# Attention, MoE 1 and MoE 2 in one kernel: MoE 2's first pass takes its weights straight from the conversion, with eight units a round and four raw buffers for a group of MoE 1's weights

## The chip, the cores and the metric

One core of a Trainium2 chip runs the whole program. The metric is the device time in microseconds of one execution. Three runs of the kernel before took 927.72, 929.70 and 931.07 us; the median is 929.7.

## The reference

Three layers run one after the other on 4 x 576 = 2304 tokens of width 512. Inputs q, k and v are float32; all weights are float64.

```
scores = q @ k.T / 8 ; half of the heads see a local window of 32, half every 32nd position
x = softmax(masked scores) @ v                       # attention, 8 heads of 64
h = x @ w_in ; x = (h * tanh(softplus(h))) @ w_out   # MoE 1, Mish, inner width 2048
g = x @ w_gate ; out = (silu(g) * (x @ w_val)) @ w_out   # MoE 2, SwiGLU, inner width 1536
```

## The kernel before, in words

**Precision.** Every large matmul is done three times (`mm3`, line 138): weights and activations are split into a high part w[:, 0] and a low part w[:, 1], and high x high, high x low and low x high are added up in PSUM.

**Conversion of a weight.** A float64 weight tile of 128 x 512 arrives as 64-bit integers (a *raw* tile, 512 KB, loaded by SyncE in `w_load`, line 213). `w_ops` (line 274) turns it into float32 with four VectorE steps a, b, c, d; ScalarE takes a Square beside them, which sends tiny values to zero. Then ScalarE casts the high part (`w_hi` or `hi_item`) and VectorE subtracts to get the low part (`w_lo` or `lo_item`). This is a *raw unit*. A *sum unit* (S12 or S34) adds and subtracts two weight tiles in two half-width VectorE steps and is split in the same way. MoE 2's tiles (keys of three parts: kind g, v or p, round, and W0, W1, S12 or S34) are written to DRAM (`wd`) after the split, and `ld` (line 1098) loads them for each round that uses them.

**Products.** With two token chunks of 512, a pass computes its products by a scheme of seven block products (`PROD`, line 683) with operands B11, T1, T2, B22, T3, B21, T4 and the weight tiles W0, S12, S34, W1. The Ts are differences of activation blocks. TensorE writes a bank, ScalarE copies products 0 to 2 aside (line 947 or 1147), and later products add to the same bank.

**MoE 1** goes through four quarters of its inner width. In quarters 1 to 3 (`middle`, line 1020) the order is: `in_round` of the first chunk pair, `small_h` of the small chunk, then `y_phase` of the two chunks (2A+1, 2A) and of the small one; then `in_round` of the second pair and its two `y_phase`. The T operands are made once in quarters 0 and 1 and written to DRAM (`td`); in quarters 2 and 3 `t_load` (line 1091) brings back those of the second pair before its `in_round`: it is issued on POOL's queue, T1 and T2 after the first quarter of the second large and of the small `y_phase`, T3 after the small one. Partial outputs are added up in DRAM (`yd`) by POOL's queue.

**What sets the order.** In attention, the list `ORDER`. In `middle`, a planner: `plan` holds the conversion units in order, with gates that say when a buffer comes free, and `fill` (line 855) emits them on VectorE wherever the engines' model clocks leave room; `need` forces a unit that TensorE is about to use. A unit's split is emitted within the next unit (`with_split`). In quarter q the plan holds four output weights of q, then some units of MoE 2 (`W2_QUARTER`), then the input weights of q + 1 with their sums. Raw tiles have two buffers (tag `raw`); each load is issued when a tile has been used. Conversions of MoE 2 write into two tiles of tag `ws`, which come free when their write to DRAM has landed.

**MoE 2** has rounds 0 to 5 on chunks 0 and 1 and the small chunk, and rounds 6 to 11 on chunks 2 and 3 (line 1318). A round is `c_round` (seven products for g and v), the output tiles of the round before (`d_tile`), and in the first six `c4_round`. 30 of the 60 conversion units of MoE 2 are left for its own rounds (`LATE_ROUND`): `w_late_step` emits one step of them after each group of matmuls. They write into four tiles of tag `wx`, go to DRAM and come back by `ld`. Their two raw tiles (`rawl`) are one half each of a tile that becomes free when MoE 1's last `in_round` is done.

Of the kernel before, what the change touches and what calls it, by code (L numbers as in the profile page):

```python
# [7 lines left out]
F32 = mybir.dt.float32  # L8
# [48 lines left out]
W2_QUARTER = (5, 5, 10, 10)  # L57
LATE_ROUND = (7, 7, 7, 8, 1)
# [46 lines left out]
def local_strided_attention__mish_moe__swiglu_kernel(  # L105
# [51 lines left out]
    w2list = []  # L157
    for i in range(NP):
        for k, kind in enumerate("gv"):
            w2list += [((kind, i, "W0"), w2[2 * i, :, k]), ((kind, i, "W1"), w2[2 * i + 1, :, k])]  # L160
            w2list += [((kind, i, "S12"), None), (("p", i, k), w2[2 * i + k, :, 2]), ((kind, i, "S34"), None)]
    wlist, plan = [], []

    def put_raw(kind, f):
        wlist.append(((kind, f), w1[f, :, "io".index(kind)]))
        plan.append(("unit",))
# [38 lines left out]
    late = {"first": len(wlist), "raw": None, "loads": 0, "units": 0}  # L205
# [7 lines left out]
    def w_load():  # L213
        i = wpos[0]
        while i < len(wlist) and wlist[i][1] is None:
            i += 1
        if i >= late["first"] and late["raw"] is None:
            return
        if i < len(wlist):
# [54 lines left out]
    def w_ops():  # L274
# [11 lines left out]
        else:  # L286
            t = sb.tile([128, 512], I32, tag="pt", name="wt2", bufs=5)
# [24 lines left out]
        raw = raws.pop(i).bitcast(I32).rearrange("p (n t) -> p n t", t=2)  # L312
        lo, hi = raw[:, :, 0], raw[:, :, 1]
        f32[key] = tf
        sq = w[:, 1].bitcast(F32) if len(key) == 2 else sb.tile([128, 512], F32, tag="sq", name="sq")
# [1137 lines left out]
```

## Time and profile before

| | before |
|---|---|
| median of three runs | 929.7 us |
| profiled execution | 927.34 us |
| span in the profile | 925.6 us |
| TensorE matmul / weight load busy | 867.8 / 715.1 us |
| VectorE / ScalarE / POOL busy | 608.0 / 455.3 / 186.6 us |
| moved by DMA | 185.47 MB, 200 GB/s in the mean |

The profile is one execution on the chip. Some 1.7 us of its time lie outside the span. PE is TensorE's matmuls, PEld its weight loads (beside them), DVE is VectorE, ACT ScalarE, SP SyncE. A queue letter (SPq, POOLq) stands for issued DMAs. L141 is line 141, the helper that emits all large matmuls, so such groups are told apart by their tiles: cX, cZ and cY are product banks, y and o output banks, h hidden ones. The clock column is the granted clock of TensorE as a share of 2.4 GHz.

### The profile page before, as it was taken

Reading aid. Unit: us, or ns where it says so; the run is one execution under the profiler, and the core shown is the slowest. Engines: PE = TensorE matmul, PEld = TensorE weight load, DVE = VectorE, ACT = ScalarE, POOL = GpSimd, SP = SyncE. Lnnn points to the kernel's source line nnn. Section 1 sums busy time; section 2 is a strip of 40 time slices with the busy share of each in tenths; the row PEclk is TensorE's granted clock in tenths of the full one; section 3 lists DMA queues with packets and bytes.
Section 4 is the critical chain, followed back from the end, with each engine's and each line's share of the span. In section 5 each row is a group of like instructions: output and inputs, shape, how many; then the busy total and the mean of one; then the engine's idle time right before and its main releaser. Section 6 shows DMA issues by size and latency. Waiting matters only on the chain.

```text
span 925.6 us, 14469 instructions
## 1 busy us (share of the span) xinstructions
PE 867.8 (94%) x5216; PEld 715.1 (77%) x5216; DVE 608.0 (66%) x1334; ACT 455.3 (49%) x1095; POOL 186.6 (20%) x216
## 2 busy tenths in 40 slices
PE   8999999989978879999795799999999999999998
PEld 5778779868856668778584678878888888888886
DVE  6998697767855746775454888978845554334434
ACT  7999846745735436564463553443424423322230
POOL 5633301001000010101113422202123321112211
PEclk9999999999998999999899799999999999999999
DMA  9855236448670495827969697898843466534422
GB/s 288 257 190 187 87 137 250 163 115 200 251 159 27 112 324 219 204 73 211 308 243 289 197 337 266 304 335 320 319 163 97 154 232 201 163 132 159 159 91 91
DMA packets 53351, 185.47 MB, mean 200 GB/s; under 512 B 5792, under 2 KB 9504, under 8 KB 50976
## 3 DMA queue, kind: packets, MB, share of 16 engines
q1 hardware_dynamic: 46512, 152.88, 47.8%
q0 software_dynamic: 6624, 31.46, 13.4%
q8 instruction: 41, 0.67, 0.3%
q14 instruction: 30, 0.25, 0.1%
q10 hardware_dynamic: 144, 0.21, 0.1%
HBM read 123.19 MB, written 61.34 MB: 199 GB/s over the span
## 4 chain that ended last, share of the span: by engine, by line
PE 63%; issue 23%; DMA 6%; DVE 4%; POOL 2%; ACT 2%; SPq 0%; POOLq 0%; DVEq 0%; ACTq 0%
PE o L141 15%; PE y L141 9%; PE cXv L141 6%; PE cXg L141 6%; PE h L141 6%; PE cZg L141 3%; PE cZv L141 3%; PE c L141 3%; PE cX L141 2%; DMA rawl<-in_w_dram 2%; PE cYg L141 2%; PE cYv L141 2%; DMA wd_v_S<-ws 1%; PE tp L501 1%; PE xp L537 1%
## 5 line engine op out<-in xcount | busy, mean ns | idle before, releaser
L141 PE MATMUL y<-g,w 128*128 128x512 f32 (+1 forms) x960 | 205.8, 372 | 8.4 <-DVE w L136 4.7
L141 PEld LDWEIGHTS y<-g,w 128*128 128x128 f32 x960 | 167.3, 190 | 41.0 <-DVE w L136 6.8
L141 PE MATMUL o<-wr,fs 128*128 128x512 f32 x648 | 149.6, 389 | 0.0
L141 PEld LDWEIGHTS o<-wr,fs 128*128 128x128 f32 x648 | 121.3, 188 | 25.0
L136 POOL TENSOR_TENSOR fs<-k,fs 128x512 fp32r<-128x512 f32 x36 | 48.8, 1355 | 252.4 <-ACT fs L131 190.5
L1211 DVE TENSOR_TENSOR acc<-acc,o 128x512 f32<-128x512 f32 x90 | 61.1, 684 | 40.2 <-PE o L141 40.2
L1006 POOL DMA_DIRECT2D yd<-yv x28 | 23.1, 823 | 310.2 <-ACT yv L1000 309.9
L136 DVE TENSOR_TENSOR ws<-wt,ws 128x512 fp32r<-128x512 f32 x60 | 43.8, 731 | 47.6 <-ACT ws L131 46.2
L131 ACT CAST ws<-wt 128x512 fp32r<-128x512 f32 x60 | 37.0, 616 | 64.3 <-DMA wd_g_W<-ws 19.2
L131 ACT CAST fs<-k 128x512 fp32r<-128x512 f32 x36 | 22.4, 622 | 85.5 <-DVE k L1164 40.6
L141 PE MATMUL h<-xh,w 128*128 128x512 f32 (+1 forms) x208 | 61.5, 360 | 0.0
L455 ACT ACTIVATE pt<-pt,sm 128x64 f32<-128x64 f32 (+1 forms) x160 | 55.8, 360 | 4.7 <-DVE sm L441 4.6
L141 PE MATMUL cXg<-T,wr 128*128 128x512 f32 x216 | 55.1, 390 | 1.9 <-ACT k L1147 1.9
L141 PE MATMUL cXv<-T,wr 128*128 128x512 f32 x216 | 54.8, 389 | 0.0
L141 PE MATMUL cX<-xT,w 128*128 128x512 f32 x144 | 41.3, 443 | 12.4 <-DMA xT<-td0T 6.2
L1000 ACT COPY yv<-y 128x512 f32<-128x512 f32 x56 | 31.5, 590 | 36.8 <-PE y L141 31.8
L141 PEld LDWEIGHTS cXg<-T,wr 128*128 128x128 f32 x216 | 40.4, 188 | 11.2 <-ACT k L1147 2.7
L141 PEld LDWEIGHTS cX<-xT,w 128*128 128x128 f32 x144 | 31.8, 223 | 20.8 <-ACT k L947 13.2
L141 PEld LDWEIGHTS cXv<-T,wr 128*128 128x128 f32 x216 | 40.5, 188 | 8.5
L1150 DVE TENSOR_TENSOR k<-cZg,k 128x512 f32<-128x512 f32 x12 | 8.3, 692 | 53.5 <-PE cZg L141 53.5
L141 PEld LDWEIGHTS h<-xh,w 128*128 128x128 f32 x208 | 37.0, 189 | 5.4 <-issue 0.4
L1147 ACT COPY k<-cXg 128x512 f32<-128x512 f32 x24 | 14.2, 590 | 48.0 <-PE cXg L141 48.0
(176 smaller groups left out, 1799.2 us busy)
## 6 DMA issues: line engine op xcount, KB each, us to landing
raw<-in_w_dram SPq DMA_DIRECT2D x50, 512.0 KB, 4.5
yd<-yv POOLq DMA_DIRECT2D x28, 512.0 KB, 7.1
wr<-wd_g_S SPq DMA_DIRECT2D x24, 512.0 KB, 4.0
wr<-wd_v_S SPq DMA_DIRECT2D x24, 512.0 KB, 5.1
wr<-wd_p SPq DMA_DIRECT2D x24, 512.0 KB, 4.7
wr<-wd_g_W SPq DMA_DIRECT2D x18, 512.0 KB, 5.3
wr<-wd_v_W SPq DMA_DIRECT2D x18, 512.0 KB, 5.9
rawl<-in_w_dram SPq DMA_DIRECT2D x18, 512.0 KB, 7.5
```

The lines of the kernel that those rows point to most:

```text
L131: nc.scalar.copy(hi, src)
L136: eng.tensor_tensor(out=lo, in0=src, in1=hi.bitcast(F32), op=ALU.subtract)
L141: nc.tensor.matmul(o, lhsT=lhs, rhs=rhs, start=first and i == 0, stop=last and i == 2, skip_group_check=more)
L455: nc.scalar.activation(out=pt[:, x], in_=pt[:, x], func=AF.Exp, scale=-1.0, bias=sm[:, 0, x:x + 1], accum_out=sm[:, 1, x:x + 1],)
L501: nc.tensor.transpose(tp[:, 128 * x:128 * x + 128], a, ident)
L537: nc.tensor.matmul(banks[r][64 * h:64 * h + 64, o:o + nq - skip], lhsT=v_t[s][rows, i, 64 * h:64 * h + 64], rhs=ts[rows, c0 + skip:c0 + nq ...
L1000: on_act(COPY if nt == 512 else 0.4, clk["pe"], lambda: nc.scalar.copy(dst, p[:, :nt]))
L1006: nc.gpsimd.dma_start(yd[c][:, e0:e + 1], src, **kw)
L1147: nc.scalar.copy(t, p)
L1150: nc.vector.tensor_tensor(out=t, in0=p, in1=t, op=ALU.add)
L1211: nc.vector.tensor_tensor(out=acc[c][:, t], in0=acc[c][:, t], in1=o, op=ALU.add)
```

## The change

MoE 2's units in MoE 1's quarters go from (5, 5, 10, 10) to (5, 2, 8, 9), and those left for its own rounds from (7, 7, 7, 8, 1) to (4, 8, 8, 8, 8). The list is put in another order: before MoE 2 begins come g and v of round 0, g of round 1 and all twelve output tiles p; left are v of round 1 and g and v of rounds 2 to 5, 18 raw units and 18 sum units. These write straight into the tiles that the next round uses (`w2_slot`): S12 and S34 have one tile for each kind, W0 and W1 two in turn by the round's parity. They still go to DRAM for the second six rounds, but `ld` doesn't load them in the first six. `w_late_flush` empties what is left at the head of a round.

Raw tiles of MoE 1's weights get four buffers for a group: the first two of tag `raw`, the other two in `ws`; such a load is issued only when all MoE 2 units before it have been split and written. Loads are now issued at the end of a unit, up to four at once (`w_load(4)`). In a group of input weights, both sums of a column pair now follow that pair.

The T loads go from POOL's queue to ScalarE's: T1 after the third quarter of the first large `y_phase`, T2 and T3 after the first and third quarter of the second. The two late raw loads are issued right after MoE 1's last `in_round`, ahead of the accumulators and of round 0's weights. Operand T4 of the first six rounds is made within MoE 1's last `y_phase` and not after round 0's first product; B11 of the second six after the first product of round 5. In attention, Square comes one step earlier, and the tiles of tag `pt` (five) and `sq` become `pt` (four) and `px` (two).

```diff
-W2_QUARTER = (5, 5, 10, 10)
-LATE_ROUND = (7, 7, 7, 8, 1)
+W2_QUARTER = (5, 2, 8, 9)
+LATE_ROUND = (4, 8, 8, 8, 8)
...
+    def w2_in(kind, i, *what):
+        k = "gv".index(kind)
+        src = {"W0": w2[2 * i, :, k], "W1": w2[2 * i + 1, :, k]}
+        return [((kind, i, x), src.get(x)) for x in what]
+
+    def w2_out(*fs_):
+        return [(("p", f // 2, f % 2), w2[f, :, 2]) for f in fs_]
+
+    w2list = w2_in("g", 0, "W0", "W1", "S12") + w2_out(0) + w2_in("g", 0, "S34") + w2_out(1, 2)
+    w2list += w2_in("v", 0, "W0", "W1", "S12") + w2_out(3) + w2_in("v", 0, "S34") + w2_out(*range(4, 11))
+    w2list += w2_in("g", 1, "W0", "W1", "S12") + w2_out(11) + w2_in("g", 1, "S34")
+    for i in range(1, NP):
+        for kind in "gv"[i == 1:]:
+            w2list += w2_in(kind, i, "W0", "W1", "S12", "S34")
...
+    def put_raw(kind, f, tag="raw"):
+        rtag[len(wlist)] = tag
...
-            put_raw("o", q * QF + f)
+            put_raw("o", q * QF + f, ("raw", "ws")[f // 2])
         if q == 1:
             plan += [("gate", ("in", 1, 0)), ("T", 1, 0), ("T", 1, 1)]
+        if q == 1:
+            n_t1 = len(wlist)
         put_w2(W2_QUARTER[q])
...
-                put_raw("i", (q + 1) * QF + 2 * cp)
-                put_raw("i", (q + 1) * QF + 2 * cp + 1)
-                put_sums(q + 1, *[("S34", 0)] * cp, ("S12", cp))
-            put_sums(q + 1, ("S34", 1))
+                put_raw("i", (q + 1) * QF + 2 * cp, ("raw", "ws")[cp])
+                put_raw("i", (q + 1) * QF + 2 * cp + 1, ("raw", "ws")[cp])
+                put_sums(q + 1, ("S12", cp), ("S34", cp))
...
+    def w_load(most=1):
+        while most:
+            i = wpos[0]
+            while i < len(wlist) and wlist[i][1] is None:
+                i += 1
+            if i >= len(wlist):
+                return
             if i < late["first"]:
-                raws[i] = sb.tile([128, 512], I64, tag="raw", name="raw", bufs=2)
+                tag = rtag.get(i, "raw")
+                if sum(rtag.get(x, "raw") == tag for x in raws) >= 2:
+                    return
+                if tag == "ws":
+                    if any(len(k) == 3 and k not in whole for k, _ in wlist[:i]):
+                        return
+                    if any(("x", P, "T4") not in whole for P in range(2 if i > n_t1 else 1)):
+                        return
+                raws[i] = sb.tile([128, 512], I64, tag=tag, name="raw", bufs=2)
             else:
+                if late["raw"] is None or late["loads"] - late["used"] >= 2:
+                    return
                 raws[i] = late["raw"][:, late["loads"] % 2]
                 late["loads"] += 1
             nc.sync.dma_start(raws[i], wlist[i][1])
-        wpos[0] = i + 1
+            wpos[0] = i + 1
+            most -= 1
...
-            tag, n = ("ws", 2) if i < late["first"] else ("wx", 4)
-            return sb.tile([128, 2, 512], F32R, tag=tag, name="ws", bufs=n)
+            if i >= late["first"]:
+                return w2_slot(key[0], key[1], key[2])
+            return sb.tile([128, 2, 512], F32R, tag="ws", name="ws", bufs=2)
...
         def a():
+            if i < n0:
+                nc.scalar.activation(out=sqo, in_=hi.bitcast(F32), func=AF.Square)
...
             wpend.append((key, w, tf))
-            w_load()
+            del raws[i]
+            if i >= late["first"]:
+                late["used"] += 1
+            if i < n0 or i >= late["first"]:
+                w_load()
...
     def w_late():
         late["raw"] = sb.tile([128, 2, 512], I64, tag="xl3", name="rawl")
-        w_load()
-        w_load()
+        w_load(2)
...
-                ops.insert(len(ops) // 2, w_hi)
-                ops.insert(len(ops) - 1, lambda: w_lo(nc.vector))
+                ops.insert(1 if len(ops) == 2 else 2, w_hi)
+                ops.insert(len(ops) - (len(ops) > 3), lambda: w_lo(nc.vector))
...
+    def w_late_flush():
+        while wq or late["units"] or wpend:
+            w_late_step()
...
         def close():
             key, w, tf = wpend.pop(0)
             behind.append((key, w, tf, lambda: end[0]))
+            w_load(4)
...
             def after1(i):
                 if i < 2:
                     late_g(q, A, i)
+                if i == 2 and q > 1:
+                    t_load(Z, "T1")
 
             def after0(i):
                 if i < 2:
                     g_make(q * NCH + 4, [2 * i, 2 * i + 1], *sm[q, i])
-                if i == 0 and q > 1:
-                    t_load(Z, "T1")
-
-            def after4(i):
-                if i == 0 and q > 1:
-                    t_load(Z, "T2")
+                if i % 2 == 0 and q > 1:
+                    t_load(Z, ("T2", "T3")[i // 2])
 
             def after3(i):
                 if i < 2:
@@ -1068,41 +1105,54 @@
 
             y_phase(q, 2 * A + 1, (0, 2, 1, 3), after1)
             y_phase(q, 2 * A, (0, 2, 1, 3), after0)
-            y_phase(q, 4, (0, 1, 2, 3), after4)
-            if q > 1:
-                t_load(Z, "T3")
+            y_phase(q, 4, (0, 1, 2, 3))
             in_round(q, Z)
             if last:
+                w_late()
                 for c in (0, 1):
                     new_acc(c, 4, 512)
                     nc.sync.dma_start(acc[c], yd[c])
-                ld(0, "S34", "W0", "S12")
+                w2_tiles("w", 6, *[(x, 0, k) if x == "W0" else (x, k) for x in ("W0", "S12", "S34") for k in "gv"])
+                ld(0, "W0", "S12", "S34")
             y_phase(q, 2 * Z + 1, (0, 2, 1, 3), after3)
             if last:
                 drain()
                 new_acc(4, 4, 256)
                 nc.sync.dma_start(acc[4], yd[4])
+                w2_tiles("ws", 2, ("W1", 0, "g"), ("W1", 0, "v"))
+                w2_tiles("raw", 2, ("p", 0), ("p", 1))
                 ld(0, "W1", 0, 1)
-                y_phase(q, 2, (0, 2, 1, 3), lambda i: [operand(0, k) for k in (("B11", "T1"), ("T2", "B22"), ("T3",), ("B21",))[i]])
+                at = (("B11", "T1"), ("T2", "B22"), ("T3", "B21"), ("T4",))
+                y_phase(q, 2, (0, 2, 1, 3), lambda i: [operand(0, k) for k in at[i]])
+                w2_tiles("wx", 4, ("W0", 1, "g"), ("W0", 1, "v"), ("W1", 1, "g"), ("W1", 1, "v"))
...
     def t_load(P, k):
         t_tile(P, k)
-        nc.gpsimd.dma_start(tops[P][k].bitcast(F32), td[P, k])
-
-    ws = {}
-    TAGS = {"W0": ("w", 6), "S12": ("w", 6), "S34": ("w", 6), "W1": ("ws", 2), 0: ("raw", 2), 1: ("raw", 2)}
-
-    def ld(r, *what):
+        nc.scalar.dma_start(tops[P][k].bitcast(F32), td[P, k])
+
+    w2t = {}
+
+    def w2_tiles(tag, n, *names):
+        for x in names:
+            w2t[x] = sb.tile([128, 2, 512], F32R, tag=tag, name="wr", bufs=n)
+
+    def w2_slot(kind, r, x):
+        if kind == "p":
+            return w2t[("W0", 0, "gv"[x]) if r == 2 * NP - 1 else ("p", x)]
+        return w2t[(x, r % 2, kind) if x[0] == "W" else (x, kind)]
+
+    def ld(r, *what, kinds="gv"):
         if r >= 2 * NP:
             return
         P, i = divmod(r, NP)
         for x in what:
-            for kind in "p" if x in (0, 1) else "gv":
-                tag, n = TAGS[x] if kind != "p" or r < 2 * NP - 1 else ("wx", 4)
-                ws[kind, r, x] = t = sb.tile([128, 2, 512], F32R, tag=tag, name="wr", bufs=n)
+            for kind in "p" if x in (0, 1) else kinds:
+                t = w2_slot(kind, r, x)
+                if kind != "p" and P == 0 and i > (kind == "g"):
+                    continue
...
         middle()
-        w_late()
         for r in range(2 * NP + 1):
             P = r // NP
-            late["units"] += LATE_ROUND[r] if r < len(LATE_ROUND) else 0
             if r in (2, 3):
                 new_acc(r, 4, 512)
                 nc.sync.dma_start(acc[r], yd[r])
             if r < 2 * NP:
+                w_late_flush()
+                late["units"] += LATE_ROUND[r] if r < len(LATE_ROUND) else 0
                 ld(r + 1, "W0")
 
                 def between(n):
-                    if r == 0 and n == 0:
-                        operand(0, "T4")
                     if r == 0 and n == 3:
                         small_operand()
                     if n == 2:
                         ld(r + 1, "S12")
                     if n == 4:
                         ld(r + 1, "S34")
-                    if r == NP - 2 and n == 6:
+                    if r == NP - 1 and n == 0:
                         operand(1, "B11")
                     if r == NP - 1 and n in (1, 3):
                         operand(1, ("T1", "T2")[n // 2])
```

## Rows read from the trace of the kernel before

**Rows 1.** Table by stage (start:end, us; busy us per engine; clock; DMA; GB/s).
```profile
163.22:222.47 59.25, 54.65 (x276) 46.07 (x276) 42.93 (x70) 32.39 (x59) 5.17 (x7) 0.97 0.49 135
...
263.30:297.57 34.27, 25.14 (x85) 18.32 (x84) 16.73 (x31) 16.30 (x28) 1.56 (x2) 0.85 0.30 65
297.57:335.54 37.97, 34.19 (x194) 29.29 (x193) 22.72 (x39) 15.54 (x29) 4.59 (x6) 1.00 0.60 175
335.54:384.96 49.42, 43.17 (x182) 35.12 (x181) 35.33 (x61) 27.53 (x51) 3.33 (x5) 0.93 0.79 245
384.96:441.00 56.04, 53.77 (x278) 44.92 (x277) 37.22 (x64) 31.43 (x56) 6.04 (x8) 1.00 0.55 149
441.00:490.45 49.45, 43.29 (x182) 35.33 (x181) 29.01 (x45) 25.38 (x47) 8.35 (x9) 0.93 0.83 268
490.45:532.96 42.51, 27.72 (x133) 23.07 (x132) 25.55 (x33) 17.88 (x33) 15.94 (x14) 0.84 0.79 241
...
611.07:651.15 40.08, 38.74 (x194) 32.73 (x193) 34.34 (x58) 16.84 (x31) 8.02 (x7) 1.00 0.90 334
```
**Rows 2.** Chain of waits, pieces without a stop (start, length, what).
```profile
129.93 10.88 PE y L141 x48
140.81 5.75 PE h L141 x48
```
**Rows 3.** Waits of TensorE in the whole span (total us, times, longest).
```profile
PE cZg L141 <- ACT k L1147: 13.9, 1, 13.9
PE cZ L141 <- ACT w L131: 8.2, 4, 3.4
PE cX L141 <- DMA xT<-td0T: 6.2, 1, 6.2
PE cX L141 <- DMA xT<-td1T: 6.2, 1, 6.2
PE y L141 <- DVE w L136: 4.7, 4, 1.5
```
**Rows 4.** Timeline of SyncE's queue, 468 to 500 us (start, length, what).
```profile
470.41 1.01 SPq L1078 DMA_DIRECT2D acc<-yd  x2
...
496.51 1.04 SPq L225 DMA_DIRECT2D rawl<-in_w_dram  x2
```
**Rows 5.** Timeline of ScalarE, 436 to 511 us (in brackets: idle before, releaser).
```profile
436.72 0.62 ACT L131 CAST ws<-wt 128x512 fp32r<-128x512 f32 x1 [8.37 <-DMA wd_g_W<-ws]
...
510.32 0.67 ACT L323 ACTIVATE sq<-rawl 128x512 f32<-128x512 f32 x1 [12.93 <-DMA rawl<-in_w_dram]
```
**Rows 6.** Timeline of VectorE, 251 to 275 us and 410 to 414 us.
```profile
251.22 0.42 DVE L319 TENSOR_SCALAR wt<-raw 128x512 int32<-128x512 int32 x1
...
272.35 0.42 DVE L300 TENSOR_TENSOR wt<-wt 128x256 f32<-128x256 f32 x1
...
274.41 0.68 DVE L136 TENSOR_TENSOR w<-wt,w 128x512 fp32r<-128x512 f32 x1
...
410.01 0.42 DVE L319 TENSOR_SCALAR wt<-raw 128x512 int32<-128x512 int32 x1
...
413.20 0.42 DVE L319 TENSOR_SCALAR wt<-raw 128x512 int32<-128x512 int32 x1
```
**Rows 7.** Timeline of POOL, 430 to 450 us.
```profile
440.25 0.89 POOL L1093 DMA_DIRECT2D xT<-td1T  x1
```
**Rows 8.** DMA issues of the whole span (count, KB each, median us to landing).
```profile
raw<-in_w_dram SPq DMA_DIRECT2D x50, 512.0 KB, 4.5
...
wd_g_W<-ws SPq DMA_DIRECT2D x12, 512.0 KB, 8.1
...
xT<-td1T POOLq DMA_DIRECT2D x3, 1024.0 KB, 13.7
```

More of the change, by code (lines that the diff above doesn't have):

```diff
@@ L154, in new_acc @@
         acc[c] = sb.tile([128, a, n], F32, tag=f"acc{c}", name=f"acc{c}")
[L157 to L164, printed above, removed]
+    def w2_in(kind, i, *what):
[10 more added lines that the diff above has]
+            w2list += w2_in(kind, i, "W0", "W1", "S12", "S34")
+    wlist, plan, rtag = [], [], {}
+    def put_raw(kind, f, tag="raw"):
+        rtag[len(wlist)] = tag
         wlist.append(((kind, f), w1[f, :, "io".index(kind)]))
@@ L199, in local_strided_attention__mish_moe__swiglu_kernel @@
             for cp in range(2):
-                put_raw("i", (q + 1) * QF + 2 * cp)
-                put_raw("i", (q + 1) * QF + 2 * cp + 1)
-                put_sums(q + 1, *[("S34", 0)] * cp, ("S12", cp))
-            put_sums(q + 1, ("S34", 1))
+                put_raw("i", (q + 1) * QF + 2 * cp, ("raw", "ws")[cp])
+                put_raw("i", (q + 1) * QF + 2 * cp + 1, ("raw", "ws")[cp])
+                put_sums(q + 1, ("S12", cp), ("S34", cp))
     assert len(w2list) == sum(LATE_ROUND)
-    late = {"first": len(wlist), "raw": None, "loads": 0, "units": 0}
+    late = {"first": len(wlist), "raw": None, "loads": 0, "used": 0, "units": 0}
     wlist += w2list
@@ L211, in local_strided_attention__mish_moe__swiglu_kernel @@
     wpos = [0, 0]
[L213 to L219, printed above, removed]
-            if i < late["first"]:
-                raws[i] = sb.tile([128, 512], I64, tag="raw", name="raw", bufs=2)
-            else:
+    whole = set()
+    def w_load(most=1):
[5 more added lines that the diff above has]
+                return
+            if i < late["first"]:
+                tag = rtag.get(i, "raw")
[7 more added lines that the diff above has]
+                raws[i] = sb.tile([128, 512], I64, tag=tag, name="raw", bufs=2)
+            else:
+                if late["raw"] is None or late["loads"] - late["used"] >= 2:
+                    return
                 raws[i] = late["raw"][:, late["loads"] % 2]
@@ L286, in w_ops @@
         else:
-            t = sb.tile([128, 512], I32, tag="pt", name="wt2", bufs=5)
+            t = sb.tile([128, 512], I32, tag="pt", name="wt2", bufs=4)
             tf = t.bitcast(F32)
@@ L311, in w_ops @@
             return [s1, s2]
-        raw = raws.pop(i).bitcast(I32).rearrange("p (n t) -> p n t", t=2)
+        raw = raws[i].bitcast(I32).rearrange("p (n t) -> p n t", t=2)
         lo, hi = raw[:, :, 0], raw[:, :, 1]
         f32[key] = tf
-        sq = w[:, 1].bitcast(F32) if len(key) == 2 else sb.tile([128, 512], F32, tag="sq", name="sq")
-        sqo = w[:, 1] if len(key) == 2 else sq
+        if len(key) == 2 or i >= late["first"]:
+            sq, sqo = w[:, 1].bitcast(F32), w[:, 1]
+        else:
+            sq = sqo = sb.tile([128, 512], F32, tag="px", name="sq", bufs=2)
         def a():
+            if i < n0:
+                nc.scalar.activation(out=sqo, in_=hi.bitcast(F32), func=AF.Square)
             nc.vector.tensor_scalar(t, hi, 3, 0x3FFFFFFF, op0=ALU.logical_shift_left, op1=ALU.bitwise_and)
@@ L322, in b @@
             nc.vector.scalar_tensor_tensor(t, lo, 29, t, op0=ALU.logical_shift_right, op1=ALU.bitwise_or)
-            nc.scalar.activation(out=sqo, in_=hi.bitcast(F32), func=AF.Square)
+            if i >= n0:
+                nc.scalar.activation(out=sqo, in_=hi.bitcast(F32), func=AF.Square)
         def c():
@@ L506, in at_copy @@
             k, n = tp.shape
-            tss[s, half] = ts = sb.tile([128, 512], F32, tag="pt", name="ts", bufs=5)[:k, :n]
+            tag, nb = ("pt", 4) if len(tss) % 6 < 4 else ("px", 2)
+            tss[s, half] = ts = sb.tile([128, 512], F32, tag=tag, name="ts", bufs=nb)[:k, :n]
             copy(ts, tp)
@@ L666, in operand @@
         if k in ("T1", "T3"):
-            tmp[k == "T3"] = [sb.tile([128, 512], F32, tag="pt", name="tt", bufs=5) for _ in range(2)]
+            tmp[k == "T3"] = [sb.tile([128, 512], F32, tag="pt", name="tt", bufs=4) for _ in range(2)]
         for j in range(2):
@@ L691, in local_strided_attention__mish_moe__swiglu_kernel @@
     ]
-    gates, floor, bg, los, whole = {}, [0.0], [], [], set()
+    gates, floor, bg, los = {}, [0.0], [], []
     yd, td, tops, sm, n6 = {}, {}, [{}, {}], {}, {}
@@ L1153, in c_round @@
                 elif k == "g":
-                    s21 = sb.tile([128, 512], F32, tag="pt", name="s21", bufs=5)
+                    s21 = sb.tile([128, 512], F32, tag="px", name="s21", bufs=2)
                     nc.scalar.activation(out=s21, in_=p, func=AF.Silu)
@@ L1175, in c4_round @@
         nt = CHUNKS[c][1]
-        s2 = sb.tile([128, 2, 256], F32, tag="pt", name="s4", bufs=5)
+        s2 = sb.tile([128, 2, 256], F32, tag="px", name="s4", bufs=2)
         for f in range(2):
```

6 lines of the change are left out of this document (3 added, 3 removed).

## The prediction

> **What bounds the kernel now.** I read TensorE's stages first, then the price of a stage without stops, then who stopped it. TensorE is the bound in most of the span: what it loses is what a change can win. In the table by stage the reader compares a stage's length with its matmuls [rows 1]. The price comes from two pieces of the chain of waits with no stop in them: 48 matmuls of 512 columns in 10.88 us, 48 of 256 columns in 5.75 us [rows 2]. A planned MoE 1 pass (`in_round`) has 84 of the first kind, 19.04 us. So the first half of a quarter (`in_round`, `small_h`, two large `y_phase`, one small) needs 19.04 + 5.75 + 21.76 + 5.75 = 52.30 us, the second half 19.04 + 21.76 = 40.80, round 0 of MoE 2 19.04 + 5.75 = 24.79, round 3 with its ten output tiles (60 matmuls) 38.39. Against that [rows 1]:
>
> - quarter 1, first half: 59.25 - 52.30 = 6.95 lost
> - quarter 2: first pass 34.27 - 19.04 = 15.23; the rest of the half 37.97 - 33.26 = 4.71; second half 49.42 - 40.80 = 8.62
> - quarter 3: 56.04 - 52.30 = 3.74 and 49.45 - 40.80 = 8.65
> - MoE 2: round 0 42.51 - 24.79 = 17.72; round 3 40.08 - 38.39 = 1.69
>
> That is 67.3 us in all, the ceiling of this change. The waits name the causes [rows 3]: one stop of 13.9 us on a ScalarE copy (round 0), 8.2 us in four stops on casts of W1 sums (`cZ <- w`, quarters 2 and 3), 6.2 us on each of two T loads (the second halves), 4.7 us on late output weights. The rest is clock: after such stops the granted clock of the stretch reads 0.85, 0.93 and 0.84 [rows 1], so part of it ran at 1.2 GHz instead of 2.4, and that goes with the stops.
>
> **The change part by part.**
>
> *Round 0: late raws loaded before everything else.* Now the two raw loads are issued at 496.51, behind the weights of round 0 [rows 4]; ScalarE's Square waits 12.93 us for them, to 510.32 [rows 5], and the copies that free TensorE's banks are queued behind it. The change issues them at the end of the last pass, ahead of the loads at 470.41 [rows 4], 26 us earlier, so the wait goes. What is late next: operand T4 moves from behind the first product's copies to in front of them. Two casts (0.62 each, as in [rows 5]) and two subtractions (about 0.68 each, the length of a split in [rows 6]) come first, 2.6 us; and the two raws, 1.05 MB at the 268 GB/s of that stretch [rows 1], push the accumulators that feed the operands back by up to 3.9 us. Product 3 then waits 2.6 to 6.5 us for a copy. I keep 4.7 of the loss: gain 13.0. Bounds: 17.7, or 4.8 if a wait as long as the 12.93 comes back elsewhere.
>
> *T loads: from POOL's queue to ScalarE's, and earlier.* Now T2 of quarter 3 is issued at 440.25 [rows 7], 0.75 before its pass begins; a T load takes 13.7 us to land [rows 8], and product 3 needs it 5.44 us into the pass. It sat behind `yd` writes, which waited for ScalarE copies, which waited 8.37 us for a weight's write-out [rows 5]. After the change T2 is issued after the first quarter of the second large `y_phase`: 8.16 + 5.75 + 5.44 = 19.35 us before its need, T1 22.07 and T3 19.35; all exceed 13.7. The six issues cost ScalarE some 0.5 us each (two issues in 1.01, [rows 4]), in `y_phase`, where ScalarE is not the bound: nothing; queued behind them are y copies and casts of g. What is late next is ScalarE's own wait for the write-out of a `ws` tile: it takes 8.1 us to land [rows 8], and with two tiles the next user comes two conversions (2 x 3.19, the distance of two equal steps in [rows 6]) later, so 1.7 us may stay in each half. Of 17.27 I take 14.0; bounds 0 (the 8.37 comes back in each) and 17.3.
>
> *MoE 1's weights.* Quarter 1 loses one raw conversion and two sums of MoE 2: 3.19 + 2 x (2 x 0.42 + 0.68) = 6.2 us of VectorE [rows 6]. The next quarter's weights, converted from 251.22 to 275.09 [rows 6], start at 245.0 and end at 268.9 at the latest. Their four raws and four sums need 4 x 3.19 + 4 x 1.52 = 18.8 of these 23.9 us; the other 5.0 are waits for raws and for ScalarE, which four buffers shorten: end between 263.8 and 268.9. The pass begins at 263.30 and wants the second S12 at 267.4 and the second S34 at 272.8: hardly a stop. Gain 13.5 of 15.23 (0 to 15.2). The output weights behind them start 8 us earlier: 3.5 of 4.71 (0 to 4.7). Quarter 2 has two sums fewer, 3.0 us: 2.5 of 3.74 (0 to 3.7).
>
> Here the change adds a wait. The third and fourth raws lie in `ws`, so SyncE's load waits for the write-out of the MoE 2 weight before it; behind it on that queue stand the other raws and write-outs, behind the conversion on VectorE the g splits that TensorE needs. Write-out plus load are 8.1 + 4.5 = 12.6 us [rows 8], less two conversions of cover, 6.4: up to 6.2 late. In quarter 1 the output weights come directly behind such a write-out, and there is nothing else to win there: -1.5, bounds -6.2 and +2 (of the 4.7 in [rows 3]). In quarters 2 and 3 the write-outs lie well before.
>
> *Rounds 1 to 4 of MoE 2.* 36 reloads of 512 KB go; of the late conversions 18 are raw and 18 sums (before 18 and 12), eight a round instead of 7, 7, 7, 8, 1. Round 3 shows the load: with eight units VectorE is busy 34.34 us [rows 1], under the 38.39 that TensorE needs; four raws and four sums are no more than its five and three. The cover is thin (4 us), and the last unit's split now stands at the head of the next round, its cast in front of the copies: 0.62 us [rows 5] in four rounds is 2.5, against the 1.69 that round 3 gives back: net -0.8, taken as -1.0; bounds +1.7 and -15.9 (below). The rounds after have no conversion and no loss to win: nothing.
>
> *The attention part*: Square one step earlier on ten units, other buffers for the same tiles. One step is 0.42 us [rows 6]: -4.2 to +4.2 us, taken as 0, since neither engine's work changes.
>
> Sum: 13.0 + 14.0 + 13.5 + 3.5 + 2.5 - 1.5 - 1.0 = 44.0. The profiled execution took 927.3 us (span 925.6), so 883.3; the median of the runs is 2.4 above it: 929.7 - 44.0 = 885.7, say **886 us**.
>
> **The rivals.**
>
> *All of it goes.* The T4 copies and the write-outs find slack: 4.7 + 3.3 + 4 of the weights' rest, 12 more: 874. For it: each stop has one named cause. Against: every one leaves a successor worked out above.
>
> *VectorE becomes the bound in rounds 1 to 4.* If every POOL instruction stops VectorE for its full length, 34.34 + 8.02 [rows 1] = 42.4 us a round against 38.39: 4.0 more in four rounds, 15.9: 902. For it: nearly all conversions and splits have two operands. Against: the 34.34 was measured with POOL at work, so the stops may be in it already. The Trainium skill, "SBUF — State Buffer", section "SBUF: two separate sides", says that VectorE instructions with two SBUF inputs and GpSimd ones that read SBUF lock each other out for a whole instruction; by that rule the sum without overlap is this rival's, while round 3's row shows no more than 34.34 busy.
>
> *MoE 1's weights stay late.* VectorE, not the raws, is what they wait for, and the planner puts other work first: 13.5 + 3.5 + 2.5 stay: 905. For it: 18.8 of 23.9 us are conversion. Against: 6.2 us less of it stands ahead.
>
> *The write-outs turn against it.* Place: SyncE's queue, at the third raw of each of the five groups after quarter 1's start (three of output weights, two of input weights). Price: with conversions starved up to 12.6 us a group, 8 at a middling cover: 40 us, and the 19.5 of the weights don't come. Remaining gain 44.0 - 19.5 - 40 = -15.5: 945. It decides from (44.0 - 19.5) / 5 = 4.9 us a group on. Against: two conversions already cover 6.4 of the 12.6, and the loads are issued a group ahead.
>
> *It doesn't do what it says*: the straight tiles are complete only when the reloads would have been, T loads wait on ScalarE for a tile: 930.
>
> **How the numbers follow.** Forecast 0.58 (its own range 875 to 898), all of it 0.10, VectorE 0.12, weights late 0.12, write-outs 0.05, nothing 0.03. Range 868 to 908: it holds the forecast, most of the next three, and leaves out the last two. A measurement here tells some 0.3% (2.8 us) from no change. Faster 0.92, same 0.03, slower 0.05.
>
> **What would show it.** Right: no `rawl` wait of ScalarE in round 0, which takes 28 to 31 us, with a stop of a few us before its third product; no `xT` line among TensorE's waits; the pass of quarter 2 at 19 to 21 us; granted clock 1.00 there; 36 fewer `wr` loads. Wrong: VectorE over 36 us busy in rounds 1 to 4 with these over 40 us long, or VectorE idle on `raw` before the third raw of a group by more than 4.9 us.

## The result, and the profile after

The changed kernel takes 892.9 us (median of 4 runs, 891.7 to 893.3) against 929.75 (927.7 to 931.1): ratio 0.9603, 95% interval 0.9584 to 0.9623. That is 36.9 us less by the medians, 35.6 by the spans of the two profiled executions (925.6 and 890.0; the profiled execution of after took 891.74). The forecast was 886, with 868 to 908 as its range.

The table by stage of the changed kernel, with the columns of [rows 1] (start:end and length, then busy us of TensorE's matmuls, its weight loads, VectorE, ScalarE and POOL, the granted clock, the busy share of the DMA engines and GB/s): first half and second half of quarters 1, 2 and 3, then rounds 0, 1 and 3 of MoE 2.

```profile
161.91:222.98 61.07, 55.50 (x279) 46.61 (x277) 42.98 (x71) 32.77 (x59) 5.17 (x7) 0.94 0.49 134
222.98:263.81 40.83, 40.83 (x183) 33.80 (x182) 31.05 (x52) 25.26 (x44) 3.34 (x5) 1.00 0.78 245
263.81:316.88 53.07, 53.06 (x277) 45.05 (x276) 36.61 (x62) 31.20 (x55) 5.04 (x6) 1.00 0.57 162
316.88:364.51 47.63, 43.48 (x182) 34.99 (x181) 33.41 (x57) 25.11 (x47) 2.61 (x3) 0.93 0.75 219
364.51:419.50 54.99, 53.21 (x278) 45.06 (x276) 36.15 (x59) 30.01 (x55) 4.13 (x5) 1.00 0.58 163
419.50:472.19 52.69, 43.94 (x183) 35.76 (x182) 29.80 (x45) 26.43 (x48) 8.75 (x9) 0.90 0.76 242
472.19:500.73 28.54, 25.35 (x134) 21.50 (x133) 24.94 (x33) 18.82 (x36) 16.58 (x14) 1.00 0.92 312
500.73:539.17 38.44, 38.44 (x194) 32.79 (x193) 33.58 (x55) 17.17 (x33) 10.59 (x9) 1.00 0.49 174
...
577.60:616.00 38.40, 38.40 (x193) 32.78 (x192) 32.80 (x55) 16.65 (x30) 8.18 (x6) 1.00 0.63 219
```

Set against [rows 1], the 35.6 us of span come from these places:

| stage | before | after | gain | forecast |
|---|---|---|---|---|
| up to quarter 1 | 163.22 | 161.91 | +1.3 | 0 |
| quarter 1, both halves | 100.08 | 101.90 | -1.8 | -1.5 |
| quarter 2, first half | 72.24 | 53.07 | +19.2 | +17.0 |
| quarter 3, first half | 56.04 | 54.99 | +1.1 | +2.5 |
| second halves of quarters 2 and 3 | 98.87 | 100.32 | -1.5 | +14.0 |
| round 0 | 42.51 | 28.54 | +14.0 | +13.0 |
| rounds 1 and later | 392.6 | 389.3 | +3.4 | -1.0 |

The miss is in the row of the second halves. The signs that the prediction named for its being right are there: 36 fewer `wr` loads of 512 KB (72 against 108), no wait of ScalarE for `rawl` in round 0, and a pass of 19.5 us at the head of quarter 2. Its signs of being wrong are not: VectorE is busy under 34 us a round, and waits at most 1.6 us for a raw of a group of MoE 1's weights (its long waits, 6.8 and 9.6 us, are for raws of MoE 2). The waits of TensorE in the whole span, beside [rows 3], say what stands there now (total us, times, longest):

```profile
PE cX L141 <- ACT k L986: 12.9, 3, 8.8
PE y L141 <- ACT w L131: 3.0, 1, 3.0
PE cXg L141 <- ACT k L1197: 2.8, 1, 2.8
PE y L141 <- DVE w L136: 2.6, 2, 1.5
PE cZ L141 <- ACT w L131: 1.8, 1, 1.8
```

The two lines of 6.2 us on a T load are gone, and so is round 0's stop of 13.9. In place of the T loads stands a line that the kernel before did not have: 12.9 us in three stops on ScalarE's copy of a first product, all in the second halves: 8.8 in quarter 3, 1.9 and 2.2 in quarter 2. Why the copy is late in quarter 3 is seen in the timeline of ScalarE of the changed kernel, 416 to 436 us (in brackets: idle before, releaser).

```profile
416.82 0.68 ACT L353 ACTIVATE sq<-raw 128x512 f32<-128x512 f32 x1 [9.97 <-DMA raw<-in_w_dram]
416.84 0.33 ACTq L1134 DMA_DIRECT2D xT<-td1T  x1
...
421.97 0.64 ACT L986 COPY k<-cX 128x512 f32<-128x512 f32 x1
433.52 0.68 ACT L353 ACTIVATE sq<-raw 128x512 f32<-128x512 f32 x1 [10.91 <-DMA raw<-in_w_dram]
434.10 0.60 ACT L131 CAST ws<-wt 128x512 fp32r<-128x512 f32 x1
434.61 0.58 ACT L986 COPY k<-cX 128x512 f32<-128x512 f32 x1
```

Read it from the bottom. The copy at 434.61 frees the bank that TensorE has waited for since 426.5. It stands behind a cast and a Square of a unit of MoE 2's weights, and that Square waits 10.91 us for its raw load. The third T load is caught in the same way at 416.84: ScalarE issues it when the Square before it lets go.

In quarter 2 the first of the two stops has another reason. The copy there stands behind a cast that waits for a write-out, and not for a raw load; only the second stop (2.2 us) goes back to a raw load.

```profile
322.19 0.62 ACT L131 CAST ws<-wt 128x512 fp32r<-128x512 f32 x1 [5.70 <-DMA wd_v_S<-ws]
...
323.77 0.62 ACT L986 COPY k<-cX 128x512 f32<-128x512 f32 x1
```

The kernel before had this wait too, hidden behind the T load. Two rows of its ScalarE and one of its TensorE, in quarter 3:

```profile
450.51 0.62 ACT L131 CAST ws<-wt 128x512 fp32r<-128x512 f32 x1 [4.94 <-DMA wd_p<-ws]
451.04 0.58 ACT L947 COPY k<-cX 128x512 f32<-128x512 f32 x1
...
452.78 5.16 PE L141 MATMUL cX<-xT,w 128*128 128x512 f32 x12 [6.16 <-DMA xT<-td1T]
```

The second half of the third product needs this copy, and it ends only 1.2 us before the T load lets TensorE go (1.6 us in quarter 2). With the T load in time and all else as it was, TensorE would still stop some 3.6 us there and 3.3 in quarter 2: an estimate, from the end of the copy less the end of the matmuls that don't need it.

So the question for quarter 3 is why the raw loads land late. SyncE's queue in the same stretch:

```profile
405.57 0.33 SPq L760 DMA_DIRECT2D wd_p<-ws  x1
405.99 0.42 SPq L248 DMA_DIRECT2D raw<-in_w_dram  x1
410.00 0.33 SPq L760 DMA_DIRECT2D wd_p<-ws  x1
410.38 0.46 SPq L248 DMA_DIRECT2D raw<-in_w_dram  x1
420.70 0.33 SPq L760 DMA_DIRECT2D wd_p<-ws  x1
421.12 0.70 SPq L248 DMA_DIRECT2D raw<-in_w_dram  x1
```

Each raw load leaves right behind a 512 KB write-out, since the change moved `w_load` from a unit's fourth VectorE operation to its `close()`, behind the `lo_item` that writes the unit before. And the DMA engines are full: the issues of 395 to 440 us (count, KB each, median us to landing), and under them the raw loads of before, 400 to 455 us:

```profile
xT<-td1T ACTq DMA_DIRECT2D x3, 1024.0 KB, 6.1
raw<-in_w_dram SPq DMA_DIRECT2D x5, 512.0 KB, 10.8
yd<-yv POOLq DMA_DIRECT2D x4, 512.0 KB, 9.6
wd_p<-ws SPq DMA_DIRECT2D x4, 512.0 KB, 9.1
```

```profile
raw<-in_w_dram SPq DMA_DIRECT2D x7, 512.0 KB, 3.7
```

The T loads now land in 6.1 us in place of 13.7 [rows 8], and the raw loads take 10.8 in place of 3.7. These two medians are not of like with like: the window of before starts 41 us ahead of its second half, that of the changed kernel 24.5. At this same distance, 416.5 to 461.5 us, before has four raw loads with a median of 8.4 us. Its loads that left from 408 to 420 us, while little else moved, took 3.4 to 3.7 us; the two issued at 431.37 and 443.32, into the full stretch, took 9.9 and 11.0. So the kernel before had slow raw loads too, two of them, where the changed kernel has four that leave after 400 us.

The theories to be told apart: **C**, contention (3 MB of T loads moved into the stretch of the raw loads); **O**, the order of issue on SyncE's queue; **R**, the T loads' second hardware queue, which takes its share from SyncE's. A fourth candidate has no run of its own, the order of the list: quarter 3's first six units of MoE 2 are now all raw units, each with a load, where they were four raw and two sum units.

### The profile page after: what moved, and what is told of

It reads as the page before. It is cut to its first block, busy times and chain, and to the rows that moved or that the text cites. A ratio compares the mean times of both kernels' runs of the same rounds, so it can differ in the third digit from the quotient of the medians.

```text
span 890.0 us, 14314 instructions
## 1 busy us (share of the span) xinstructions
PE 858.8 (96%) x5216; PEld 711.9 (80%) x5216; DVE 612.6 (69%) x1334; ACT 455.8 (51%) x1095; POOL 187.2 (21%) x210
## 3 DMA queue, kind: packets, MB, share of 16 engines
q0 software_dynamic: 5760, 25.17, 11.7%
## 4 chain that ended last, share of the span: by engine, by line
PE 79%; DMA 8%; DVE 6%; ACT 4%; issue 1%; SPq 0%; POOL 0%; ACTq 0%; DVEq 0%; POOLq 0%
PE o L141 17%; PE y L141 14%; PE h L141 7%; PE cXg L141 7%; PE cXv L141 7%; PE cX L141 6%; DMA raw<-in_w_dram 5%; PE cZg L141 4%; PE c L141 3%; PE cZv L141 3%; PE cZ L141 3%; PE cYg L141 2%; PE cYv L141 2%; PE cY L141 2%; PE xp L575 1%; PE tp L538 1%
## 5 line engine op out<-in xcount | busy, mean ns | idle before, releaser
L141 PE MATMUL cX<-xT,w 128*128 128x512 f32 x144 | 38.6, 418 | 12.9 <-ACT k L986 12.9
L141 PEld LDWEIGHTS cXg<-T,wr 128*128 128x128 f32 x216 | 40.4, 188 | 11.7 <-ACT k L1197 3.2
L141 PEld LDWEIGHTS cX<-xT,w 128*128 128x128 f32 x144 | 28.6, 201 | 20.5 <-ACT k L986 14.5
L521 POOL TENSOR_TENSOR pt<-pt,sm 128x192 f32<-128x192 f32 (+2 forms) x48 | 34.1, 730 | 16.6 <-DVE sm L514 13.0
L141 PE MATMUL h<-xl,w 128*128 128x512 f32 (+1 forms) x104 | 36.4, 350 | 0.0
```

The lines of the kernel that those rows point to most:

```text
L141: nc.tensor.matmul(o, lhsT=lhs, rhs=rhs, start=first and i == 0, stop=last and i == 2, skip_group_check=more)
L521: nc.gpsimd.tensor_tensor(out=a, in0=a, in1=sm[:, 1, x].unsqueeze(2).to_broadcast(a.shape), op=ALU.mult)
```

## The experiments

Ratios are to the kernel before, run beside each; the changed kernel's is 0.9603. One thing on precision: the same code for quarter 2's second half took 43.9, 46.2 and 44.9 us in three kernels that differ only elsewhere (e4_t_first, g2_mix, g3_mix_t4), so differences of a second half under 2.5 us are not read.

**e1_no_t: no T loads.** The tiles of the other pair of chunks are used again, so part of the products has wrong operands.

```
-        t_tile(P, k)
-        nc.scalar.dma_start(tops[P][k].bitcast(F32), td[P, k])
+        tops[P][k] = tops[1 - P][k]
```

> The changed kernel without the six loads of T1, T2 and T3 in quarters 2 and 3: the tiles of the other pair of chunks are used again, so part of the products has wrong operands, while every instruction of TensorE, VectorE and ScalarE is as before. Theory C (the 1 MB T loads, moved ahead into the first half's last 20 us, share the DMA engines with the raw weight loads, which land late, and ScalarE's Squares that wait for them hold up the products' copies): raw loads land in 4 to 6 us in place of 10.8, the stops of TensorE behind a first product's copy (4.2 us in quarter 2, 8.8 in quarter 3) go, the second halves fall from 47.6 and 52.7 to 41 to 42 us: about 875 us (872 to 880). Theory O (raw loads are issued too late, behind the write-outs on SyncE's queue and with only two buffers, whatever else is on the DMA engines): the stops stay, 888 to 893 us.

Measured: 886.2 us, ratio 0.9537 [0.949, 0.9584]. Between the two theories. The second halves by stage:

```profile
318.82:361.85 43.03, 41.43 (x182) 33.63 (x181) 31.15 (x53) 24.46 (x46) 2.79 (x4) 1.00 0.73 209
416.12:465.14 49.02, 42.77 (x182) 34.91 (x181) 27.98 (x42) 24.48 (x43) 7.66 (x7) 0.93 0.77 242
```

Quarter 2 loses 2.2 us to its 40.8 (its floor, the length without stops) in place of 6.8: contention was most of it. Quarter 3 still loses 8.2 in place of 11.9, with no T traffic at all. The four raw loads that leave after 400 us land in 9.9 us (the same four of the changed kernel in 11.2), among four units of the form `p` in a row, each with a 512 KB write-out ahead of the next load. C alone doesn't do.

**e2_raw_d: the raw load ahead of the write-out again**, at the fourth VectorE operation.

```
-            if i < n0 or i >= late["first"]:
-                w_load()
+            w_load(1 if i < n0 or i >= late["first"] else 4)
```

> The changed kernel with the raw load of MoE 1's units issued where it was before the change, at the unit's fourth VectorE operation, ahead of the previous unit's write-out on SyncE's queue, and not at the unit's end behind it. Theory O: the raw loads leave 1 to 2 us earlier each, the second halves give back 4 to 8 us: 884 to 889 us. Theory C: the loads leave earlier but into the same full DMA engines, less than 2 us: 890 to 893 us.

Measured: 887.9 us, ratio 0.9561 [0.9524, 0.9598]. Quarter 3's second half falls from 52.69 to 49.32, quarter 2's stays (47.58 against 47.63):

```profile
317.02:364.60 47.58, 44.32 (x183) 35.35 (x181) 34.44 (x58) 26.58 (x50) 4.17 (x6) 0.93 0.77 225
419.00:468.32 49.32, 44.22 (x183) 35.66 (x181) 28.34 (x43) 25.16 (x47) 7.66 (x7) 0.93 0.78 251
```

So O holds in quarter 3. The raw loads take the same 10.8 us, but leave earlier, and ScalarE's waits for them in 380 to 445 us shrink from 20.9 to 9.4 us; against that, 9.5 us of waits for the `wd_p` write-outs appear, which now land later (11.5 in place of 9.1).

**e3_t_pool: the T loads at their new places, on POOL's queue** (`nc.gpsimd.dma_start` in place of `nc.scalar.dma_start`).

> The changed kernel with the T loads at their new places but issued on POOL's queue, as before the change, and not on ScalarE's. Theory C: the same 3 MB in the same stretch, now also in line with POOL's accumulations: no gain, and TensorE's waits for a T tile may come back: 890 to 900 us. Theory R (ScalarE's queue as a further hardware queue takes its share from SyncE's raw loads; and the third T load is issued late since ScalarE itself waits): raw loads land in about 5 us again, 880 to 886 us.

Measured: 894.6 us, ratio 0.963 [0.9595, 0.9666], not to be told from the changed kernel. Second halves 47.4 and 54.0 us, and the raw loads of 395 to 440 us land as late:

```profile
raw<-in_w_dram SPq DMA_DIRECT2D x5, 512.0 KB, 11.7
```

R falls: for the raw loads it doesn't matter which queue carries the megabytes. (The T loads themselves took 13.1 us from POOL's queue and 6.1 from ScalarE's.) The Trainium skill ("DMA: Bandwidth & Descriptors", section "Issuing engines are not separate DMA queues") says that DMAs of ScalarE, SyncE and GpSimd end on the same 16 engines and interleave there; 11.7 against 10.8 us agrees.

**e4_t_first: the three T loads right after the seven products**, on ScalarE's queue, where the T tiles' slots have just been read for the last time.

```
+            if q > 1:
+                for k in TSLOT:
+                    t_load(Z, k)
             small_h(q)
...
-                if i == 2 and q > 1:
-                    t_load(Z, "T1")
...
-                if i % 2 == 0 and q > 1:
-                    t_load(Z, ("T2", "T3")[i // 2])
```

> The changed kernel with all three T loads issued on ScalarE's queue at the end of the first half's seven products, before chunk 4's product, some 11 us earlier for T1 and 30 for T3: the DMA engines moved nothing between 380 and 394 us there. Theory C: 3 MB leave in about 10 us before the raw loads and accumulations begin; the second halves fall to 41 to 44 us each: 876 to 882 us. Theory O: the raw loads are as late as before, 888 to 893 us.

Measured: 885.0 us, ratio 0.9522 [0.9483, 0.9562]. In quarter 3 the three loads leave at 384.06 to 385.34, after a stretch in which the DMA engines moved nothing, and land in 7.9 us. (In the changed kernel this stretch ends at 388 us with a raw load, and not at 394 as expected.) The second halves:

```profile
317.93:361.82 43.89, 41.46 (x182) 33.64 (x181) 31.36 (x54) 23.32 (x43) 2.62 (x3) 1.00 0.74 214
417.64:463.87 46.23, 42.75 (x183) 34.84 (x181) 27.05 (x42) 24.17 (x43) 7.66 (x7) 0.96 0.80 256
```

3.7 us less in quarter 2's second half, 6.5 in quarter 3's; the 876 to 882 of theory C were missed by 3 us, since the part that is O's stays. Why quarter 3 is 2.8 us shorter here than with no T loads at all is open; the four raw loads that leave after 400 us landed in 8.9 us here and in 9.9 there.

**f3_both: e2_raw_d and e4_t_first together.**

> The two edits that helped together: all three T loads right after the seven products, and the raw load issued at the unit's fourth VectorE operation, ahead of the write-out. If they take away different parts of the raw loads' lateness (contention, and the place in SyncE's queue behind a 512 KB write-out): 878 to 882 us, second halves of 42 to 45 us. If both only shorten the same wait, so that the second finds nothing left: 883 to 886 us.

Measured: 881.4 us, ratio 0.9495 [0.9466, 0.9524]: the two take away different parts in quarter 3, whose second half is now 1.2 us from its floor. This rests on the stage; the interval of the whole time overlaps that of e4_t_first.

```profile
319.14:366.33 47.19, 43.47 (x183) 35.44 (x181) 33.75 (x56) 26.10 (x47) 2.82 (x4) 0.93 0.72 203
419.87:461.92 42.05, 41.13 (x183) 33.72 (x182) 25.76 (x40) 23.76 (x43) 7.67 (x7) 1.00 0.74 235
```

Quarter 2's second half reads 47.2: there ScalarE waits 8.3 and 6.6 us for write-outs of `ws` tiles (6.2 and 3.2 in e4_t_first), which now stand behind the raw loads. But the code of e4_t_first itself took up to 46.2 us there, so that this order costs anything in quarter 2 is not shown.

**f1_two_raw: MoE 1's groups through two raw buffers**, as before the change.

```
-        rtag[len(wlist)] = tag
+        rtag[len(wlist)] = "raw"
```

> The changed kernel with MoE 1's groups of four weights read into the two buffers named raw alone, as before the change, and no raw load in the buffers named ws. Theory of the four buffers (quarter 2's first half lost its 19 us of stops because all four raw weights of a group are in flight at once): the stops come back in that half, 60 to 72 us for it in place of 53.1, 898 to 911 us in all. Rival (it is quarter 1's shorter list, two units of MoE 2's in place of five, that lets quarter 2's weights begin in time): that half stays below 56 us, 890 to 896 us.

Measured: 894.3 us, ratio 0.9631 [0.96, 0.9661]. The first half of quarters 1 and 2:

```profile
161.53:223.03 61.50, 55.08 (x279) 46.26 (x277) 42.98 (x71) 32.67 (x59) 5.17 (x7) 0.94 0.50 133
...
263.86:316.95 53.09, 53.08 (x277) 45.05 (x276) 35.68 (x60) 30.01 (x54) 5.05 (x6) 1.00 0.62 178
```

Neither stage moves: 53.09 against 53.07, 61.50 against 61.07. The four buffers give nothing that can be measured, and cost nothing. That leaves the shorter list of quarter 1 for quarter 2's 19 us, which the next two runs test from the other side; the new order of the sums within a group was not tried alone.

**f4_both_3: three units of MoE 2 in quarter 1, eight in quarter 3** (`W2_QUARTER = (5, 3, 8, 8)`), on f3_both.

> As f3_both, with one unit of MoE 2's list taken in quarter 1 that stood in quarter 3 (3, 8 and 8 units in place of 2, 8 and 9): 0.5 MB less to read and 0.5 to 1 MB less to write in quarter 3, where the raw loads are late. If DMA volume there sets the second half: 1 to 3 us below f3_both. If the quarter is at its floor already, or quarter 1 with its T tiles has no room: 0 to 2 us above it.

Measured: 899.5 us, ratio 0.9684 [0.964, 0.9729], 18 us above f3_both and outside both expectations. Quarter 2's first half alone went from 53.30 to 67.10:

```profile
268.44:335.54 67.10, 59.00 (x277) 47.77 (x276) 41.19 (x71) 33.81 (x61) 5.05 (x6) 0.92 0.57 166
```

One conversion of 3.2 us costs 13.8. VectorE stands 5.93 us for the third unit's raw load (to 239.65), so quarter 2's weights come later by more than the unit itself. From VectorE's timeline, the splits that complete the first of them and the last of its sums, in f3_both and, below, here:

```profile
251.91 0.69 DVE L136 TENSOR_TENSOR w<-wt,w 128x512 fp32r<-128x512 f32 x1
...
269.90 0.69 DVE L136 TENSOR_TENSOR w<-wt,w 128x512 fp32r<-128x512 f32 x1 [0.70 <-ACT w L131]
```

```profile
258.89 0.69 DVE L136 TENSOR_TENSOR w<-wt,w 128x512 fp32r<-128x512 f32 x1 [0.73 <-ACT w L131]
...
279.57 0.68 DVE L136 TENSOR_TENSOR w<-wt,w 128x512 fp32r<-128x512 f32 x1
```

7.0 us later at the start, 9.7 at the end, for a pass that begins only 2.6 us later (268.44 against 265.84). It stops five times on such casts and splits, and the granted clock of 268 to 300 us reads 0.84.

**g4_three_two: the same with two raw buffers**, to see whether the loads in `ws` buffers, which wait for the third unit's write-out, were the price.

> As f4_both_3 (three units of MoE 2 in quarter 1), with the groups of MoE 1's weights read through the two buffers named raw alone. If quarter 2's first half took 67 us there since the raw loads in the buffers named ws wait for the third unit's write-out: 53 to 57 us for it here, 881 to 886 us in all. If the third unit itself fills VectorE's time ahead of quarter 2's weights: 65 to 72 us still, 895 to 903 us.

Measured: 904.7 us, ratio 0.9736 [0.9703, 0.9769].

```profile
265.18:334.59 69.41, 59.14 (x278) 47.51 (x277) 40.58 (x70) 33.33 (x61) 5.05 (x6) 0.93 0.57 158
```

69.4 us: not the buffers. It is the length of the list ahead of quarter 2's weights.

**f2_late_late: the late raw loads back behind round 0's loads** (`w_late()` after `middle()`).

> The changed kernel with the first two raw loads of MoE 2's late units issued again where the rounds begin, on SyncE's queue behind the loads of the accumulators and of round 0's weights, and not at the end of the last quarter's products. Theory of the early raws (they alone give round 0's gain): round 0 stops again at its third or fourth product, 36 to 42 us in place of 28.5, 900 to 906 us in all. Rival (the gain is from the later T4 and from fewer units in round 0, four in place of seven): round 0 stays below 32 us, 892 to 896 us.

Measured: 899.4 us, ratio 0.9684 [0.9649, 0.9719]. Round 0 takes 36.21 us in place of 28.54, and ScalarE's row is that of [rows 5] again, at half the length:

```profile
489.21 0.67 ACT L353 ACTIVATE wr<-rawl 128x512 fp32r<-128x512 f32 x1 [6.33 <-DMA rawl<-in_w_dram]
```

The place of these two loads is worth 7.7 us of the stage here. The wait is 6.33 and not 12.93, since the loads leave 3.95 us into the round (6.06 before), and land 11.2 us after issue (13.8 before).

**g1_before_raws: the kernel before with the late raw loads alone moved ahead** (`w_late()` right after `drain()`, which is one `y_phase` later than in the change).

> The kernel before with one edit of the change alone: the first two raw loads of MoE 2's late units issued once the last of MoE 1's list is done, ahead of the last accumulator's and of W1's loads, some 15 us earlier. Theory of the early raws: ScalarE's wait of 12.93 us in round 0 is gone or under 2 us, the round falls from 42.5 to 28 to 32 us: 917 to 921 us. Rival (round 0's gain needs the whole change: fewer units there, T4 earlier, the loads issued earlier): the wait only shrinks to some 6 us, as when the loads were put back in the changed kernel: 922 to 927 us.

Measured: 918.3 us, ratio 0.9895 [0.9859, 0.9931], 9.3 us less than the 927.6 of the kernel before beside it. Round 0:

```profile
491.85:521.81 29.96, 27.01 (x133) 22.50 (x132) 25.41 (x33) 17.78 (x33) 15.97 (x14) 0.94 0.97 329
```

12.5 us off the round by one moved call: the early raws do it without the rest of the change. The round begins 1.4 us later than before, so the span gains 10.9.

**g2_mix: the earlier raw load in quarter 3 alone, on e4_t_first.**

> The T loads right after the seven products, as in e4_t_first, and the raw load at the fourth VectorE operation for the units of quarter 3 alone, where that helped (second half 42.1 us in f3_both), while quarters 1 and 2 keep it at the unit's end (second half 43.9 us in e4_t_first against 47.2 in f3_both). If each quarter keeps what it had in the run that it is taken from: 883 - 4 - 2 = 876 to 879 us. If the quarters hang together, so that a faster second quarter brings quarter 3's raw loads into another stretch: 880 to 884 us.

Measured: 881.0 us, ratio 0.9484 [0.9453, 0.9515], the same as f3_both. Quarter 3's second half kept its gain (42.48 us), quarter 2's took 46.16 and not 43.9 with the same code: the 2 us that were to be saved are within what that stage varies by itself.

**g3_mix_t4: g2_mix with T4 behind the first product's copies.**

> As g2_mix, with round 0's operand T4 made behind the first product's copies, as in the kernel before, and not ahead of them. If T4's two casts and two subtractions in front of the copies make the stop of 2.8 us ahead of the third product: it goes, 2.5 to 4 us below g2_mix. Rival (the stop is the accumulator's chain or the output copies in front, which stay): within 1 us of g2_mix.

Measured: 879.1 us, ratio 0.9467 [0.9433, 0.9502]. TensorE's stop ahead of the third product:

```profile
469.46 1.67 PE L141 MATMUL cXg<-T,wr 128*128 128x512 f32 x6 [0.91 <-ACT k L1198]
```

From 2.81 to 0.91 us, and round 0 from 30.16 to 27.47: T4 in front of the copies makes the stop. In the whole time the step, 1.9 us, is within the measurement. This is the fastest version, about 13 us below the changed kernel (0.9467 against 0.9603, of 929.75).

## Why the prediction was right, and where it was wrong

**T loads and second halves: forecast +14.0, measured -1.5. This is the step that failed.** The forecast costed the T loads by their own landing (13.7 us against 19.35 of lead), and that part came true: no `xT` wait is left. It went wrong in two ways. First, it kept 1.7 us a half for the next wait, ScalarE's for a `ws` write-out. This wait is the right one in quarter 2 (5.70 us at 322.19), but the trace of before already had it, with some 3.3 and 3.6 us of stop behind the T load by the estimate above, about twice the 1.7. Second, it left out what the moved loads land on. It took 4.5 us for a raw load, the median of the whole span [rows 8], as given, although the stage rows already had the DMA engines at 0.79 and 0.83 of their time in the second halves [rows 1]. T1, T2 and T3 brought 3 MB into 397 to 423 us, where the raw loads of the units of MoE 2 are due. And it did not price a moved step at all: `w_load` went from a unit's fourth operation to its end, which puts each raw load behind a write-out of 512 KB. e1_no_t and e4_t_first show the contention (3.7 to 4.6 us in quarter 2, though the code of e4_t_first gave only 1.5 and 2.7 in g2_mix and g3_mix_t4; 3.7 to 6.5 in quarter 3), e2_raw_d the order (3.4 in quarter 3), f3_both that in quarter 3 they add up, from 52.7 to 42.05. In all, the stops and the lower clock behind them were 6.8 and 11.9 us, where 1.7 a half were forecast. In quarter 3 the wait is for a raw load, which the forecast did not name. How much the new order of the list adds to it is not shown; without touching it, f3_both comes within 1.2 us of the floor.

**Round 0: forecast +13.0, measured +14.0, for the reason given.** g1_before_raws gives 12.5 by the early loads alone; f2_late_late takes back 7.7 of the 14.0, and what gives the rest there was not taken apart. The successor named in advance, T4 in front of the copies with 2.6 to 6.5 us at product 3, is the 2.80 of the waits; g3_mix_t4 takes it away.

**MoE 1's weights: forecast +17.0 and +2.5, measured +19.2 and +1.1.** Right in size. Of the two reasons given, 6.2 us less of VectorE ahead of them and four raw buffers, only the first stands: two buffers give the same 53.09 us, one unit more in quarter 1 gives 67.1 and three more, two of them sums (the kernel before), 72.24.

**Quarter 1: forecast -1.5, measured -1.8, right by luck and for a wrong reason.** The raw loads in `ws` buffers were to cost it; with two raw buffers it is 61.50. What costs the 8.8 us over its floor there, 5.6 of them stops on the output weights, was not tried. With it falls the rival in which the write-outs turn against the change: f1_two_raw and g4_three_two show no price of those buffers.

**Rounds 1 to 4: forecast -1.0, measured +3.4 for all rounds behind round 0.** VectorE is busy 32.80 us of round 3 and POOL 8.18, and the round takes 38.40, its floor. The rival of 902 us added the two; their sum is 41.0 here, and the round is shorter than that. The Trainium skill ("SBUF — State Buffer", section "SBUF: two separate sides") says that VectorE instructions with two SBUF inputs and GpSimd ones that read SBUF shut each other out for a whole instruction; whether VectorE's busy time holds such stops can't be seen in this row, but they don't lengthen the round. The splits at the head of the next round cost nothing that TensorE sees.

The sum missed by 8.4 us of the span's 35.6: the failed step is 15.5 too high, the others together 7.1 too low. That the total came as near as 7 us to the 886 is in part luck: nearly half of the error was made up by terms that have nothing to do with it.

## What to carry to other kernels

When a load is moved earlier, list every other transfer that is due in the new stretch, and price those, not only the moved one: here the T loads came in time and the raw loads paid. Look also at the wait that ends just before the one you remove: here a copy came 1.2 us ahead of the T load, and by the estimate above more than half of the stop was its own. ScalarE's rows show that an operation that waits for a load holds all that is behind it (a Square 10.91 us, with the copy behind it), so the price of a late load is read at the copies queued behind its Square. And a call that changes its place in the code by one operation changes its place in a queue: look at which transfer it now stands behind.

## What the runs showed beyond that

- A stage with no slack multiplies: one unit of 3.2 us more in quarter 1 cost quarter 2's first half 13.8 us, by a raw load that landed late, weights 7 to 10 us behind, and a granted clock of 0.84 over 31.6 us.
- With loads, write-outs and accumulating writes together, the DMA engines moved 271 to 309 GB/s at 0.97 and 1.04 of their time (419.5 to 435.5 us of after, 441 to 457 of before), and a load of 512 KB took 11 to 12 us, where the loads of before that left from 408 to 420 us took 3.4 to 3.7.
